# Two dense layers in float32 on one core: the second layer's products in seven block products for eight

## The chip, the cores and the metric

The kernel runs on one core of a Trainium2 chip. The metric is the device time of one execution in microseconds (us). An execution consists of one program on five engines: TensorE (PE, with the weight loads listed apart as PEld), VectorE (DVE), ScalarE (ACT), GpSimd (POOL, not used here) and SyncE (SP, which issues all the DMAs).

## The reference

Chunked attention with a few memory keys makes 3072 rows of 512 numbers; two dense layers with different activations follow. Only the second of them is touched by the change.

```python
x = attention(q, k, v, mem_k, mem_v)          # (3072, 512)
h = x @ moe_w_in                              # (3072, 2048)
g = h * (1.0 / (1.0 + np.exp(-1.702 * h)))
x = g @ moe_w_out                             # (3072, 512)
h = x @ moe2_w_in                             # (3072, 2048)
g = np.maximum(h, 0.0) + alpha * np.minimum(h, 0.0)
return (g @ moe2_w_out).astype(np.float32)    # (3072, 512)
```

The layers' weights and alpha arrive as float64.

## The kernel before

**Precision.** A float32 product is made of three products of numbers in the short format fp32r: each operand is split into a high part (a cast on ACT) and a low part (the difference, on DVE), and high x high, high x low and low x high are added in PSUM. So each block product costs three matmuls, and each operand that a product reads costs one cast and one subtraction. The matmuls that carry the time have 128x128 weights and 512 columns.

**Steps.** `steps` (lines 426 to 434) lists 192 steps: 6 blocks of 512 tokens by 16 chunks `f` of 128 hidden units in the first layer, and the same in the second. A step is `mm1` (12 matmuls into `h`, line 334), the activation (`act1`, lines 342 and 343, or `act2`, lines 348 and 349), `split_g` (lines 355 and 356), and one step later the second product: `mm2_t` (line 364) in the first layer, `mm2_n` (line 374) in the second, 12 matmuls into the PSUM pairs `ya` and `yb`. So a step of either layer has 24 matmuls, and the second layer has 2304. Attention for later tokens is spread over the first five blocks of the first layer (`attend`).

**Weights.** All 16 chunks of a layer stand in SBUF. A chunk comes by two DMAs as float64 (`w_load`), ACT takes the absolute value (`w_abs`, line 98), DVE builds the float32 out of the bits in four operations (`w_bits`, lines 106 to 115), then comes the split into high and low (`w_high`, line 126, `w_low`, line 131). The second layer's chunks are prepared in the last block of the first layer and shortly after it (lines 531 to 535), each into the buffers of a chunk of the first layer that is no longer used.

**Between the layers.** The first layer's result goes to DRAM (`y1`); the second layer loads blocks of 512 tokens of it (`load_y`) and splits them (`split_y`, lines 422 and 423). At the end of a block `finish2` moves the four accumulators out of PSUM and stores the rows.

**Order.** The code is written in program order; a scheduler of the framework then sets each engine's own order when the program is built. An engine works strictly down its own list, and waits where an operand isn't ready.

Of the kernel before, what the change touches and what calls it, by code (L numbers as in the profile page):

```python
# [9 lines left out]
F32 = mybir.dt.float32  # L10
# [21 lines left out]
P2_BLOCKS = [512] * 6  # L32
TBM = 512
# [12 lines left out]
NACC = (4, 5, 6, 7)  # L46
F64_TINY = float(np.uint32(0x38000000).view(np.float32))
# [4 lines left out]
def fused_kernel(ctx: ExitStack, tc: tile.TileContext, qs, ks, vs, ident, w_in1, w_out1, w_in2, w_out2, alpha, out):  # L52
# [3 lines left out]
    wp = ctx.enter_context(tc.tile_pool(name="wp", bufs=NF - 2 - NWB))  # L56
    wr = ctx.enter_context(tc.tile_pool(name="wr", bufs=2))
    xp = ctx.enter_context(tc.tile_pool(name="xp", bufs=2))
# [8 lines left out]
    y1 = dr.tile([NKC, 128, NT], F32, name="y1")  # L67

# [5 lines left out]
    pieces = [(p, f) for p in (1, 2) for f in range(NF)]  # L74
# [6 lines left out]

    def w_load(s):
        p, f = pieces[s]
        wi, wo = (w_in1, w_out1) if p == 1 else (w_in2, w_out2)
# [34 lines left out]
    def w_high(s):  # L119
        p, f = pieces[s]  # L120
        if f >= NF - 2 and "wp" not in side:
            side_stack.close()
            side["wp"] = side_stack.enter_context(tc.tile_pool(name="wp2", bufs=2, side="right"))
        pool = side["wp"] if f >= NF - 2 else side["wpb"] if f >= NF - 2 - NWB else wp
        wt[p, f] = [pool.tile([128, 2, 512], F32R, tag=t, name=f"{t}{p}_{f}") for t in ("whi", "wlo")]
        nc.scalar.copy(wt[p, f][0].rearrange("p i n -> p (i n)"), wst[s][1].bitcast(F32))  # L126
# [34 lines left out]


# [125 lines left out]
    def a_xcopy(m):  # L288
        tok = m * SQ
        b = int(np.searchsorted(p1_start, tok, side="right")) - 1  # L290
        if b not in xt:
            xt[b] = xp.tile([128, 2, NKC, TBM], F32R, tag="x", name=f"x{b}")
# [53 lines left out]
    def act2(h, n, f):  # L346
        t = gp.tile([128, TBM], F32, tag="t", name="t")
        nc.vector.tensor_scalar(out=t[:, :n], in0=h[:, :n], scalar1=0.0, scalar2=al_sb[:, f:f + 1], op0=ALU.min, op1=ALU.mult)  # L348
        nc.vector.scalar_tensor_tensor(out=t[:, :n], in0=h[:, :n], scalar=0.0, in1=t[:, :n], op0=ALU.max, op1=ALU.add)  # L349
        return t  # L350
# [18 lines left out]
    def mm2_n(p, y, gs, n, f):  # L369
        gh, gl = gs  # L370
        wh, wl = wt[p, f]
        for m in range(n // 128):
            for i, (g, w) in enumerate(((gh, wh), (gh, wl), (gl, wh))):
                mm = nc.tensor.matmul(  # L374
                    y[m], g[:, m * 128:(m + 1) * 128], w[:, 1, :],
                    start=(f == 0 and i == 0), stop=(f == NF - 1 and i == 2),
                )
                if ahead_done and f == NF - 1:
                    tc.keep_in_program_order(mm)

# [9 lines left out]
    def finish2(y, t0, n):  # L390
        last = t0 + n == NT
        if last:
            wide = ph2["pool"].tile([128, NKC, TBM], F32, tag="yraw", name="olast")
        for m in range(n // 128):
            o = wide[:, m] if last else op.tile([128, DM], F32, tag="o", name="o2")
            rows = out[t0 + m * 128:t0 + (m + 1) * 128, :]
            if last and m == n // 128 - 1:
                c = DM // 2
                nc.vector.tensor_copy(o[:, :c], y[m][:, :c])
                nc.scalar.copy(o[:, c:], y[m][:, c:])  # L400
                nc.sync.dma_start(out=rows[:, :c], in_=o[:, :c])
                nc.sync.dma_start(out=rows[:, c:], in_=o[:, c:])
                continue
            if m % 2:
                nc.scalar.copy(o, y[m])
            else:
                nc.vector.tensor_copy(o, y[m])
            nc.sync.dma_start(out=rows, in_=o)

    yraw = {}  # L410
    ph2 = {}

    def load_y(j):
        t0, n = j * P2_BLOCKS[0], P2_BLOCKS[j]
        t = ph2["pool"].tile([128, NKC, TBM], F32, tag="yraw", name=f"yraw{j}")
        nc.sync.dma_start(out=t, in_=y1[:, :, t0:t0 + n].rearrange("k p t -> p k t"))
        yraw[j] = t

    def split_y(j):
        t = yraw.pop(j)  # L420
        x = xp.tile([128, 2, NKC, TBM], F32R, tag="x", name=f"yx{j}")
        nc.scalar.copy(x[:, 0], t)
        nc.vector.tensor_tensor(out=x[:, 1], in0=t, in1=x[:, 0].bitcast(F32), op=ALU.subtract)
        xt[100 + j] = x
# [6 lines left out]
    t0 = 0  # L431
    for j, n in enumerate(P2_BLOCKS):
        steps += [(2, j, t0, n, f) for f in range(NF)]
        t0 += n
# [5 lines left out]
    ahead = []  # L440
    ahead_done = []
# [41 lines left out]
    side["wpb"] = ctx.enter_context(tc.tile_pool(name="wpb", bufs=NWB))  # L483
# [4 lines left out]
    def do_mm2(i):  # L488
# [13 lines left out]
    for i, (p, j, t0, n, f) in enumerate(steps):  # L502
# [83 lines left out]
```

## Time and profile before

| | |
|---|---|
| median of 3 runs | 1164.79 us (1162.69 to 1165.32) |
| the profiled execution: time | 1164.72 us |
| its span | 1162.9 us |
| TensorE busy | 1135.7 us, 98% of the span |
| VectorE busy | 590.6 us, 51% |
| ScalarE busy | 315.1 us, 27% |

The span counts from the first to the last thing that the profiler saw of the program; 1.8 us lie around it. Shares of busy time are means over stages: until about 150 us attention starts and the first layer's weights are prepared; until about 540 us the first layer and attention run side by side; from 540 to about 690 us the second layer's weights are prepared; from then on only the second layer runs. A matmul's recorded duration is longer than the distance to the next one, since matmuls are pipelined; distances are taken from start times.

### The profile page before, as it was taken

Reading aid. Unit: us, or ns where it says so; the run is one execution under the profiler, and the core shown is the slowest. Engines: PE = TensorE matmul, PEld = TensorE weight load, DVE = VectorE, ACT = ScalarE, POOL = GpSimd, SP = SyncE. Lnnn points to the kernel's source line nnn. Section 1 sums busy time; section 2 is a strip of 40 time slices with the busy share of each in tenths; the row PEclk is TensorE's granted clock in tenths of the full one; section 3 lists DMA queues with packets and bytes.
Section 4 is the critical chain, followed back from the end, with each engine's and each line's share of the span. In section 5 each row is a group of like instructions: output and inputs, shape, how many; then the busy total and the mean of one; then the engine's idle time right before and its main releaser. Section 6 shows DMA issues by size and latency. Waiting matters only on the chain.

```text
span 1162.9 us, 17787 instructions
## 1 busy us (share of the span) xinstructions
PE 1135.7 (98%) x7804; PEld 922.4 (79%) x7804; DVE 590.6 (51%) x848; ACT 315.1 (27%) x519; POOL 0.2 (0%) x4
## 2 busy tenths in 40 slices
PE   5799999999999999999999999999999999999998
PEld 4677778878878887888877888888888888888886
DVE  5899644343434333343799865334334434444443
ACT  3566432232222222223444321111111111111111
POOL 0000000000000000000000000000000000000000
PEclk6799999999999999999999999999999999999999
DMA  8754222121113112214444501001100100100001
GB/s 296 249 173 166 79 80 67 43 79 46 60 41 103 43 46 76 62 43 136 162 173 145 181 1 37 37 1 37 37 1 1 37 1 1 37 1 1 36 1 37
DMA packets 44382, 82.74 MB, mean 71 GB/s; under 512 B 5137, under 2 KB 21905, under 8 KB 44305
## 3 DMA queue, kind: packets, MB, share of 16 engines
q1 hardware_dynamic: 44304, 81.61, 20.8%
q8 instruction: 61, 1.00, 0.4%
q14 instruction: 17, 0.13, 0.0%
HBM read 69.02 MB, written 12.58 MB: 70 GB/s over the span
## 4 chain that ended last, share of the span: by engine, by line
PE 83%; DVE 8%; DMA 4%; ACT 2%; issue 1%; SPq 1%; DVEq 0%; ACTq 0%
PE h L334 40%; PE yb L374 11%; PE ya L374 11%; PE ya L364 9%; PE yb L364 8%; DMA wraw<-w_out 4%; PE xp L282 2%; DVE wtmp L112 2%; DVE wtmp L115 2%; PE sc L204 1%; DVE wlo L131 1%; DVE wtmp L106 1%; ACT wtmp L98 1%; DVE wtmp L109 1%; DVE gl L356 1%
## 5 line engine op out<-in xcount | busy, mean ns | idle before, releaser
L334 PE MATMUL h<-x,whi 128*128 128x512 f32 x768 | 244.6, 396 | 3.3 <-ACT whi L126 1.9
L355 ACT CAST gh<-t 128x512 fp32r<-128x512 f32 x192 | 119.0, 621 | 452.0 <-DVE t L349 329.0
L334 PE MATMUL h<-yx,whi 128*128 128x512 f32 x768 | 238.5, 390 | 0.0
L356 DVE TENSOR_TENSOR gl<-t,gh 128x512 fp32r<-128x512 f32 x192 | 132.3, 689 | 111.7 <-ACT gh L355 110.2
L334 PEld LDWEIGHTS h<-x,whi 128*128 128x128 f32 x768 | 143.3, 189 | 35.8 <-ACT whi L126 2.6
L348 DVE TENSOR_SCALAR t<-h,al_sb 128x512 f32<-128x512 f32 x96 | 71.9, 749 | 192.9 <-PE h L334 192.9
L334 PEld LDWEIGHTS h<-yx,whi 128*128 128x128 f32 x768 | 144.2, 188 | 30.9
L334 PE MATMUL h<-x,wlo 128*128 128x512 f32 x384 | 151.4, 394 | 0.0
L343 DVE SCALAR_TENSOR_TENSOR t<-t,h 128x512 f32<-128x512 f32 x96 | 65.8, 685 | 168.6 <-ACT t L342 168.3
L334 PE MATMUL h<-yx,wlo 128*128 128x512 f32 x384 | 149.8, 390 | 0.0
L342 ACT ACTIVATE t<-h 128x512 f32<-128x512 f32 x96 | 57.3, 598 | 187.2 <-PE h L334 186.9
L334 PEld LDWEIGHTS h<-x,wlo 128*128 128x128 f32 x384 | 72.4, 189 | 16.0 <-DVE wlo L131 0.4
L334 PEld LDWEIGHTS h<-yx,wlo 128*128 128x128 f32 x384 | 72.1, 188 | 15.5
L364 PE MATMUL ya<-gl,whi 128*128 128x512 f32 x192 | 77.2, 402 | 0.0
L364 PE MATMUL ya<-gh,whi 128*128 128x512 f32 x192 | 76.4, 398 | 0.3 <-ACT gh L355 0.3
L364 PE MATMUL yb<-gh,wlo 128*128 128x512 f32 x192 | 75.5, 393 | 0.0
L364 PE MATMUL yb<-gl,whi 128*128 128x512 f32 x192 | 75.4, 393 | 0.0
L364 PE MATMUL yb<-gh,whi 128*128 128x512 f32 x192 | 75.4, 393 | 0.0
L364 PE MATMUL ya<-gh,wlo 128*128 128x512 f32 x192 | 75.1, 391 | 0.0
L374 PE MATMUL ya<-whi,gh 128*128 128x512 f32 x192 | 74.9, 390 | 0.0
L374 PE MATMUL yb<-whi,gl 128*128 128x512 f32 x192 | 74.9, 390 | 0.0
L374 PE MATMUL yb<-whi,gh 128*128 128x512 f32 x192 | 74.9, 390 | 0.0
(67 smaller groups left out, 1298.2 us busy)
## 6 DMA issues: line engine op xcount, KB each, us to landing
wraw<-w_in SPq DMA_DIRECT2D x32, 512.0 KB, 4.0
wraw<-w_out SPq DMA_DIRECT2D x32, 512.0 KB, 4.9
v<-vs SPq DMA_DIRECT2D x24, 512.0 KB, 3.7
k<-ks SPq DMA_DIRECT2D x24, 416.0 KB, 4.5
q<-qs SPq DMA_DIRECT2D x24, 256.0 KB, 3.0
y<-o SPq DMA_DIRECT2D x24, 256.0 KB, 2.3
yraw<-y SPq DMA_DIRECT2D x6, 1024.0 KB, 5.3
out<-o SPq DMA_DIRECT2D x20, 256.0 KB, 2.1
```

What stands on the lines that cost most here:

```text
L98: i = nc.scalar.activation(out=a.bitcast(F32), in_=wst[s][0][:, :, 1].bitcast(F32), func=AF.Abs)
L112: nc.vector.scalar_tensor_tensor(out=a, in0=top, scalar=0xC0000000, in1=a, op0=ALU.bitwise_and, op1=ALU.bitwise_or)
L115: nc.vector.scalar_tensor_tensor(out=a, in0=low, scalar=29, in1=a, op0=ALU.logical_shift_right, op1=ALU.bitwise_or)
L282: nc.tensor.matmul(x[half[z], g, j, c * CHUNK:(c + 1) * CHUNK], s["v"][half[g], c, 2 * j + z, :], s["p"][half[g], 2 * z + j // 2, b * CHUN ...
L334: nc.tensor.matmul(h[:, :n], w[:, 0, k * 128:(k + 1) * 128], x[:, z, k, :n], start=(i == 0), stop=(i == 3 * NKC - 1))
L342: nc.scalar.activation(out=t[:, :n], in_=h[:, :n], func=AF.Tanh, scale=1.702 / 2)
L343: nc.vector.scalar_tensor_tensor(out=t[:, :n], in0=t[:, :n], scalar=1.0, in1=h[:, :n], op0=ALU.add, op1=ALU.mult)
L348: nc.vector.tensor_scalar(out=t[:, :n], in0=h[:, :n], scalar1=0.0, scalar2=al_sb[:, f:f + 1], op0=ALU.min, op1=ALU.mult)
L355: nc.scalar.copy(gh[:, :n], g[:, :n])
L356: lo_eng.tensor_tensor(out=gl[:, :n], in0=g[:, :n], in1=gh[:, :n].bitcast(F32), op=ALU.subtract)
L364: nc.tensor.matmul(y[m][:, :n], w[:, 1, m * 128:(m + 1) * 128], g[:, :n], start=(f == 0 and i == 0), stop=(f == NF - 1 and i == 2),)
L374: mm = nc.tensor.matmul(y[m], g[:, m * 128:(m + 1) * 128], w[:, 1, :], start=(f == 0 and i == 0), stop=(f == NF - 1 and i == 2),)
```

## The change

The second layer runs over 3 pairs of 512-token blocks (1024 tokens) in place of 6 blocks. Both its products are cut into 2x2 blocks and made by Strassen's method in seven block products, `p1` to `p7`, where eight were needed. This takes sums and differences of blocks of both operands ahead of the products, and sums of products behind them.

- **Weights** (`c_load` to `c_store`): during blocks 2 to 4 of the first layer, 16 units (8 of `w_in2`, 8 of `w_out2`) of four 128x256 blocks are loaded, converted as before, turned into seven combinations (four sums `s1` to `s4` of 128x256), split, and stored in DRAM (`wi2`, `wo2`). A unit's work is spread over three steps (`PSTEP`). The preparation in the last block of the first layer falls away.
- **Tokens** (`x_load`, `x_sum`, `x_split`): four blocks of `y1` make seven left operands per pair by four subtractions, seven casts and seven low parts. For pairs 1 and 2 these 11 steps are put between the products of the second product of the pair before (`fill`).
- **First product** (`first`): per pair 8 chunk pairs `fp` x 7 products x 6 matmuls. Accumulators `x`, `y`, `z` take up several products one after the other; ACT copies intermediate values out (`snap`), DVE adds them to the later ones, and the activation runs in SBUF.
- **Second product** (`second`): per pair 7 products x 4 quarters `jj` x 12 matmuls. `r_make` makes an operand for each (product, quarter): for p5, p6, p7 and p4 a subtraction of 128x1024 in place (lines 596 to 602), then a cast on ACT (line 605) and a low part on DVE (line 606), two quarters ahead of the product (`RLEAD`), into a ring of four slots.
- **Weights again** (`s_ahead`): the combinations are read from DRAM anew for each pair, in 60 units of up to 512 KB, ten units ahead.
- The output is written transposed and turned on the host.

```diff
-P2_BLOCKS = [512] * 6
+PAIR = 1024
...
+    def c_bits(u):
+        raw, oa = prep[u]
+        top, low, a, af = raw[:, :, :, 1], raw[:, :, :, 0], oa[:, :, 1].bitcast(U32), oa[:, :, 1].bitcast(F32)
+        nc.vector.tensor_scalar(out=af, in0=af, scalar1=F64_TINY, scalar2=F64_HUGE, op0=ALU.max, op1=ALU.min)
...
+    def c_sums(u):
...
+        for o, x, y, fn in ((s1, a21, a22, ALU.add), (s2, s1, a11, ALU.subtract), (s3, a11, a21, ALU.subtract),
+                            (s4, a12, s2, ALU.subtract)):
+            nc.vector.tensor_tensor(out=o, in0=x, in1=y, op=fn)
+        prep[u] += ob
+        for t in (oa[:, 1:4], ob[0], ob[1]):
+            nc.scalar.copy(t[:, :, 0], t[:, :, 1].bitcast(F32))
...
+    PRODUCTS = ("p1", "p5", "p6", "p3", "p7", "p2", "p4")
...
+    def x_sum(P, n):
+        x, y = {"p7": ("p3", "p5"), "p5": ("p5", "p1"), "p6": ("p3", "p5"), "p4": ("p2", "p6")}[n]
+        nc.vector.tensor_tensor(out=xraw[n], in0=xraw[x], in1=xraw[y], op=ALU.subtract)
...
+        nc.scalar.copy(hi, r)
+        nc.vector.tensor_tensor(out=lo, in0=r, in1=hi.bitcast(F32), op=ALU.subtract)
...
+            nc.sync.dma_start(out=t.bitcast(F32), in_=src)
...
+            w = units[P, "a", fp, d // 2][:, d % 2]
+            hi, lo = xops[P][n]
+            i = 0
+            for k in range(2):
+                for c, x in ((0, hi), (0, lo), (1, hi)):
+                    nc.tensor.matmul(
+                        to, w[:, c, k * 128:(k + 1) * 128], x[:, k], start=(i == 0 and n not in ADDED), stop=(i == 5),
...
+                with_, f, th = {"p3": ("u2", fp, 1), "p7": ("s5", fp + NFP, 1), "p2": ("s1", fp, 0), "p4": (None, fp + NFP, 0)}[n]
+                out = graw[f // 2, th][:, f % 2]
+                if with_ is not None:
+                    nc.vector.tensor_tensor(out=out, in0=to, in1=kept[with_], op=ALU.add)
+                    to = out
+                act2(out, to, f)
...
+    def r_make(P, d, jj):
...
+        if n == "p5":
+            nc.vector.tensor_tensor(out=b11, in0=b12, in1=b11, op=sub)
+        elif n == "p6":
+            nc.vector.tensor_tensor(out=b11, in0=b22, in1=b11, op=sub)
+        elif n == "p7":
+            nc.vector.tensor_tensor(out=b12, in0=b22, in1=b12, op=sub)
+        elif n == "p4":
+            nc.vector.tensor_tensor(out=b11, in0=b21, in1=b11, op=sub)
...
+        hi, lo = r_slot(P, f"r{P}_{d}_{jj}_")
+        nc.scalar.copy(hi, src)
+        nc.vector.tensor_tensor(out=lo, in0=src, in1=hi.bitcast(F32), op=sub)
...
+            for ahead in order[(0 if q == 0 else q + RLEAD):q + RLEAD + 1]:
+                r_make(P, *ahead)
+            if fill and q >= 4 and q % 2 == 0:
+                fill.pop(0)()
...
-        q = i - last1 - LAG
-        if q >= 0:
-            goal = NPC + 1 + (q * 3) // 4
-            while wtick[0] < min(2 * NPC + 1, goal):
-                w_tick(2 * NPC)
...
+        u, r = divmod(i - PREP0, PSTEP)
+        for v in (u, u - 1):
+            k = r + PSTEP * (u - v)
+            if 0 <= v < 2 * NFP and k < len(PREP):
+                for fn in PREP[k]:
+                    fn(v)
```

What this does to the order is shown at three places. In each row the line is that of the kernel it belongs to, then come the output, the inputs and the shape; numbers behind names tell buffers apart.

VectorE, in the first layer beside attention, before: `t` is the activation of a step, `gl` its low part, `x4` a low part of attention's result.

```order
L343 SCALAR_TENSOR_TENSOR t_3728<-t_3728,h1_3715 128x512
L356 TENSOR_TENSOR gl_3732<-t_3728,gh_3731 128x512
L343 SCALAR_TENSOR_TENSOR t_3767<-t_3767,h1_3754 128x512
L356 TENSOR_TENSOR gl_3771<-t_3767,gh_3770 128x512
L297 TENSOR_TENSOR x4_3613<-xp17_3786,x4_3613 128x2x4x64
```

VectorE, the same stage after: `t` and `gl` are lines 416 and 428, `oa11` is unit 11 of the weights (lines 199 to 206), `mx13`, `ex13` and `sm13` belong to attention's softmax.

```order
L416 SCALAR_TENSOR_TENSOR t_2875<-t_2875,h1_2862 128x512
L199 TENSOR_SCALAR oa11_4759<-oa11_4759 128x4x256
L428 TENSOR_TENSOR gl_2879<-t_2875,gh_2878 128x512
L298 TENSOR_REDUCE mx13_2826<-sc13_2793 128x8
L200 TENSOR_SCALAR oa11_4759<-oa11_4759 128x4x256
L306 TENSOR_TENSOR ex13_2827<-sc13_2793,mx13_2826 128x512
L203 SCALAR_TENSOR_TENSOR oa11_4759<-raw11_4709,oa11_4759 128x4x256
L325 TENSOR_REDUCE sm13_2830<-ex13_2827 128x8
L206 SCALAR_TENSOR_TENSOR oa11_4759<-raw11_4709,oa11_4759 128x4x256
L328 TENSOR_SCALAR sm13_2830<-sm13_2830 128x8
L416 SCALAR_TENSOR_TENSOR t_2923<-t_2923,h1_2910 128x512
```

Between the activation of one step and that of the next now stand four operations of 1024 columns of a weights' unit.

VectorE, in the second layer before: three operations a step, one after the other.

```order
L348 TENSOR_SCALAR t_7675<-h2_7662,al_sb_82 128x512
L349 SCALAR_TENSOR_TENSOR t_7675<-h2_7662,t_7675 128x512
L356 TENSOR_TENSOR gl_7679<-t_7675,gh_7678 128x512
L348 TENSOR_SCALAR t_7707<-h2_7694,al_sb_82 128x512
L349 SCALAR_TENSOR_TENSOR t_7707<-h2_7694,t_7707 128x512
```

VectorE, in pair 0 after, where the first product ends and the second begins: `g` are the activations, `acc7` the accumulator of the last chunk pair, `xr1` the token operands of pair 1 (`fill`), `r0_2_0` and `r0_2_1` the low parts for quarters 0 and 1 of p6; the two `rx` rows are those for quarter 2 of p6 and, last, for quarter 3 of p1.

```order
L478 TENSOR_TENSOR xr1p7_6825<-xr1p3_6824,xr1p5_6822 128x1024
L606 TENSOR_TENSOR r0_2_0_1_6953<-g0_0_0_6198,r0_2_0_0_6952 128x1024
L422 SCALAR_TENSOR_TENSOR g0_7_1_6213<-g0_7_1_6213,t_6793 128x512
L422 SCALAR_TENSOR_TENSOR g0_3_0_6204<-g0_3_0_6204,t_6804 128x512
L606 TENSOR_TENSOR r0_2_1_1_6973<-g0_1_0_6200,r0_2_1_0_6972 128x1024
L478 TENSOR_TENSOR xr1p5_6822<-xr1p5_6822,xr1p1_6821 128x1024
L602 TENSOR_TENSOR g0_0_0_6198<-g0_4_0_6206,g0_0_0_6198 128x1024
L421 TENSOR_SCALAR t_6815<-acc7_6747,al_sb_82 128x512
L606 TENSOR_TENSOR rx_6820<-g0_2_0_6202,rx_6820 128x1024
L602 TENSOR_TENSOR g0_1_0_6200<-g0_5_0_6208,g0_1_0_6200 128x1024
L606 TENSOR_TENSOR rx_6820<-g0_3_0_6204,rx_6820 128x1024
```

The low part for p1's last quarter stands behind three of p6, two subtractions for p4 and two sums for the next pair.

TensorE, in the second layer before: second products of one chunk, then first products of the chunk after the next.

```order
L374 MATMUL yb_7054<-whi2_12_5965,gh_7408 128x512
L374 MATMUL yb_7054<-wlo2_12_5966,gh_7408 128x512
L374 MATMUL yb_7054<-whi2_12_5965,gl_7409 128x512
L334 MATMUL h2_7456<-yx2_6696,whi2_14_6087 128x512 x2
L334 MATMUL h2_7456<-yx2_6696,wlo2_14_6088 128x512
```

TensorE, in pair 0 after, at the same place as the VectorE rows: the first row is quarter 2 of p5, lines 557 are the last product (p4) of the first product, `u35` is the weights' unit of p1's last quarter, `r0_2_0` is p6.

```order
L629 MATMUL acc9_6919<-rx_6820,u38_6764 128x512 x7
L557 MATMUL acc7_6747<-xw0_1_5937,u31_6638 128x512
L557 MATMUL acc7_6747<-xlo0p4_6159,u31_6638 128x512
L557 MATMUL acc7_6747<-xw0_1_5937,u31_6638 128x512 x2
L557 MATMUL acc7_6747<-xlo0p4_6159,u31_6638 128x512
L557 MATMUL acc7_6747<-xw0_1_5937,u31_6638 128x512
L629 MATMUL acc9_6919<-rx_6820,u38_6764 128x512 x5
L629 MATMUL acc8_6842<-rx_6820,u35_6711 128x512 x12
L629 MATMUL acc8_6842<-r0_2_0_0_6952,u40_6807 128x512
```

TensorE comes to p1's last quarter right behind three quarters of p5, and all of p6 stands behind it.

## Rows read from the trace of the kernel before

**Rows 1.** The page: busy us, share of span and instructions of each engine.

```profile
PE 1135.7 (98%) x7804; PEld 922.4 (79%) x7804; DVE 590.6 (51%) x848; ACT 315.1 (27%) x519; POOL 0.2 (0%) x4
```

**Rows 2.** Windows: busy us and count by engine, PE clock, DMA share, GB/s.

```profile
50.00:150.00 100.00, 97.56 (x790) 75.26 (x786) 86.03 (x116) 56.17 (x116) 0.00 (x0) 1.00 0.43 143
350.00:400.00 50.00, 50.00 (x462) 40.68 (x461) 21.28 (x40) 14.21 (x24) 0.00 (x0) 1.00 0.25 78
700.00:800.00 100.00, 100.00 (x441) 82.32 (x440) 42.50 (x59) 14.69 (x22) 0.00 (x0) 1.00 0.06 22
```

**Rows 3.** The chain that ended last: same place in two second-layer blocks (start, us).

```profile
726.70 5.48 PE h L334 x24
814.19 5.48 PE h L334 x24
```

**Rows 4.** The same chain: the same place in two first-layer blocks.

```profile
299.47 3.85 PE h L334 x17
398.80 3.85 PE h L334 x17
```

**Rows 5.** Timeline of PE (start, us) in the last block of the first layer.

```profile
598.10 0.39 PE L364 MATMUL yb<-gh,wlo 128*128 128x512 f32 x1
598.84 0.73 PE L334 MATMUL h<-x,whi 128*128 128x512 f32 x2 [0.36 <-DVE t L343]
...
620.94 0.40 PE L334 MATMUL h<-x,wlo 128*128 128x512 f32 x1
622.37 0.73 PE L334 MATMUL h<-x,whi 128*128 128x512 f32 x2 [1.03 <-DVE t L343]
```

**Rows 6.** Groups by line and shape: count, busy us, mean ns, idle before, releaser.

```profile
L356 DVE TENSOR_TENSOR gl<-t,gh 128x512 fp32r<-128x512 f32 x192 | 132.3, 689 | 111.7 <-ACT gh L355 110.2 <-ACT whi L126 1.1
L348 DVE TENSOR_SCALAR t<-h,al_sb 128x512 f32<-128x512 f32 x96 | 71.9, 749 | 192.9 <-PE h L334 192.9
L131 DVE TENSOR_TENSOR wlo<-wtmp,whi 128x1024 fp32r<-128x1024 f32 x32 | 38.9, 1217 | 0.6 <-ACT whi L126 0.5
L106 DVE TENSOR_SCALAR wtmp<-wtmp 128x1024 f32<-128x1024 f32 x32 | 22.0, 689 | 21.0 <-ACT wtmp L98 20.7
```

**Rows 7.** Timeline of DVE where its list never runs dry.

```profile
599.31 1.22 DVE L131 TENSOR_TENSOR wlo<-wtmp,whi 128x1024 fp32r<-128x1024 f32 x1
600.44 1.22 DVE L112 SCALAR_TENSOR_TENSOR wtmp<-wraw,wtmp 128x1024 uint32<-128x1024 uint32 x1
601.58 0.69 DVE L356 TENSOR_TENSOR gl<-t,gh 128x512 fp32r<-128x512 f32 x1
602.18 0.68 DVE L343 SCALAR_TENSOR_TENSOR t<-t,h 128x512 f32<-128x512 f32 x1
```

**Rows 8.** Windows around the fall and the rise of PE's clock.

```profile
4.00:6.00 2.00, 0.98 (x66) 0.72 (x64) 0.14 (x2) 0.00 (x0) 0.00 (x0) 1.00 0.89 270
6.00:8.00 2.00, 0.00 (x0) 0.00 (x0) 1.41 (x3) 0.48 (x1) 0.00 (x0) 0.85 0.98 302
8.00:10.00 2.00, 0.00 (x0) 0.00 (x0) 0.86 (x2) 0.14 (x1) 0.00 (x0) 0.50 1.03 392
...
44.00:46.00 2.00, 2.00 (x8) 1.62 (x7) 2.00 (x4) 0.00 (x0) 0.00 (x0) 0.77 0.00 0
```

**Rows 9.** Timeline of PE ahead of that rise.

```profile
41.26 1.63 PE L334 MATMUL h<-x,whi 128*128 128x512 f32 x3
42.69 0.63 PE L334 MATMUL h<-x,wlo 128*128 128x512 f32 x1
43.12 1.05 PE L334 MATMUL h<-x,whi 128*128 128x512 f32 x2
```

**Rows 10.** Windows: stretches with much DMA traffic.

```profile
10.00:12.00 2.00, 0.00 (x0) 0.00 (x0) 0.00 (x0) 1.12 (x1) 0.00 (x0) 0.50 1.03 412
640.00:650.00 10.00, 10.00 (x46) 8.28 (x45) 6.53 (x9) 2.03 (x3) 0.00 (x0) 1.00 0.74 260
585.00:600.00 15.00, 14.64 (x65) 11.73 (x64) 13.79 (x17) 8.78 (x12) 0.00 (x0) 1.00 0.52 172
```

More of the change, by code (lines that the diff above doesn't have):

```diff
@@ L388, in finish1 @@
             nc.sync.dma_start(out=y1[m, :, t0:t0 + n], in_=o[:, :n])
[L390 to L402, printed above, removed]
-                continue
[L404 to L408, printed above, removed]
@@ new lines, in s_done, with two_banks, g_alloc, snap @@
+    def s_done(n):
+        streamed[1] += n
+        s_ahead(streamed[1] + 10)
+    npair = [0]
+    def two_banks():
+        t = pair(("a", "ya", "yb")[npair[0] % 3], f"acc{npair[0]}")
+        npair[0] += 1
+        return t
+    graw = {}
+    def g_alloc(P):
+        for j in range(NFP):
+            for th in range(2):
+                graw[j, th] = chunk_slot(6 + 2 * (j % 4) + j // 4, th, DIM, F32, f"g{P}_{j}_{th}")
+    def snap(src, tag, name):
+        t = gp.tile([128, TBM], F32, tag=tag, name=name, bufs=2)
+        nc.scalar.copy(t, src)
+        return t
@@ L426, in fused_kernel @@
+    late = {}
+    ringx = []
     steps = []
@@ L529, in fused_kernel @@
             attend(j, 2 * f + 2)
-        q = i - last1 - LAG
-        if q >= 0:
-            goal = NPC + 1 + (q * 3) // 4
-            while wtick[0] < min(2 * NPC + 1, goal):
-                w_tick(2 * NPC)
-        if i == last1 + 6:
-            split_y(0)
-            load_y(1)
-        if p == 2 and f == 6 and j + 1 < len(P2_BLOCKS):
-            split_y(j + 1)
-            if j + 2 < len(P2_BLOCKS):
-                load_y(j + 2)
-    for i in range(len(steps) - LAG, len(steps)):
-        do_mm2(i)
+        u, r = divmod(i - PREP0, PSTEP)
[4 more added lines that the diff above has]
+                    fn(v)
+        if i == last1 + 2:
+            x_load(0)
+            fill = x_steps(0)
+        if i >= last1 + 4 and fill:
+            fill.pop(0)()
+        if last1 + 4 <= i:
+            s_ahead(i - last1 - 4)
+    s_ahead(10)
+    for P in range(NPAIR):
+        g_alloc(P)
+        for fp in range(NFP):
+            first(P, fp, (lambda: do_mm2(len(steps) - 1)) if P == 0 and fp == 0 else None)
+        if P == 0:
+            ringx.append(xp.tile([128, 2, 2, 2, TBM], F32R, tag="x1", name="rx"))
+        fill = []
+        if P + 1 < NPAIR:
+            x_load(P + 1)
+            fill = x_steps(P + 1)
+        second(P, fill)
+        npair[0] += 1
+        while fill:
+            fill.pop(0)()
 def _layout(q, k, v, mem_k, mem_v):
```

265 lines of the change are left out of this document (206 added, 59 removed).

## Prediction

> **What bounds the kernel now.** I read the page's first part, then the windows by stage, then the chain that ended last, then single instructions. TensorE is busy for 98% of the span, VectorE for 51% [rows 1]. The share is a mean, so the stages count: from 350 to 400 us and from 700 to 800 us TensorE is never idle at its full clock, and VectorE is busy for 43% of each [rows 2]. The chain of waits says the same: the piece of line 334 with 24 matmuls that starts at 726.70 comes again at 814.19 [rows 3], so a block of the second layer takes 87.49 us for 16 x 24 = 384 matmuls, 0.2278 us each, and nothing else stands between them. A block of the first layer takes 99.33 us [rows 4]; what it has beyond that is attention's matmuls. The second layer thus goes by the number of its matmuls: 2304 x 0.2278 = 524.8 us. TensorE waits for VectorE only where the second layer's weights are prepared [rows 5].
>
> **The part removed.** Seven products for eight: per pair, the first product has 8 x 7 x 6 = 336 matmuls, the second 7 x 4 x 12 = 336; three pairs make 2016. 288 fewer, all with 512 columns and a new 128x128 weight load as now, at 0.2278 us: **-65.6 us**. They go entirely, since TensorE is the bound there. Left are 459.2 us.
> [...]
>
> The second layer's preparation leaves the last block of the first layer. There TensorE lost time twice: from 598.10 to 598.84 and from 620.94 to 622.37, where a matmul's step is 0.23 [rows 5], so 0.51 + 1.20 = **-1.7 us** (0 if the eleven steps for pair 0's token operands, now at that place, cost as much).
>
> **The part moved: weights in the first layer.** A unit costs VectorE four operations for the bits, four sums of 256 columns and three low parts. Two-input operations of 1024 columns last 1.217 us, of 512 columns 0.689, single-input ones of 1024 columns 0.689 [rows 6]; where the list is full, each starts 0.09 before the one ahead has ended: 1.13 us from start to start for 1024 columns, 0.60 for 512 [rows 7]. So 2 x 1.13 + 2 x 0.60 for the bits, 4 x 0.4 for the sums (estimated by the line through 512 and 1024 columns), 0.87 + 2 x 0.60 for the low parts: 7.1 us. A unit takes three steps, 3 x 99.33 / 16 = 18.6 us, in which VectorE already does 43% [rows 2], 8.0 us: together 15.1, 81%. The 16 units fill 49 steps, 304 us. In the order, a unit's operations stand between the activation of one step and that of the next, where TensorE has the second product of the step before as cover, 12 matmuls or 2.7 us. Nearest row: from 50 to 150 us VectorE was busy for 86%, and TensorE idle for 2.44 of 100 us [rows 2], with the first layer's weights prepared in the same way. So 0 to 7.4 us in 304; I take **+3 us**. ACT's and SP's share (3.2 us of casts, and 2.8 MB per unit in the queue ahead of attention's loads) lies beside it.
>
> **The part added in the first product.** Per chunk pair TensorE has 42 matmuls, 9.57 us. VectorE has three sums, four first and four second operations of the activation, 3 x 0.60 + 3 x 0.40 + 0.66 + 4 x 0.60 = 6.1 us. (0.40 is an estimate for a 512-column single-input operation in SBUF with a scalar per row: half of what line 106 does, and the 0.06 by which line 348 is longer than a plain one; from PSUM line 348's 0.749 less 0.09 [rows 6].) TensorE's order interleaves three chunk pairs, so a wait for a sum has four or more products of 1.37 us in between. Cost nothing; if the cover fails, some 0.3 us each, inside the range.
>
> **The part added in the second product.** This decides. Over a pair VectorE has 28 low parts and 16 subtractions of 1024 columns, and in pairs 0 and 1 eleven more for `fill`: 55 x 1.13 = 62 us, with eight evictions 67, beside 76.5 us of TensorE. The sum fits, but not everywhere. Take the stretch from the first matmul of p1 to p1's last quarter. TensorE passes 36 matmuls of p1, 24 of the first product's end and 36 of p5, and one with the high part, before it needs the low part: 97 x 0.2278 = **22.1 us**. VectorE's list up to that low part (the last row of the fourth order shown), counted from the subtraction for p5's quarter 2, is 34 operations: 17 of 1024 columns, 3 sums, 7 second and 5 first operations of the activation, and 2 first ones from PSUM: 17 x 1.13 + 10 x 0.60 + 5 x 0.40 + 2 x 0.66 = **28.5 us**. It starts about 1.2 us before p1 does: the four operations ahead of it, 2.7 us, follow on the end of p3 of chunk pair 6, 18 matmuls before p1. So the low part comes at 28.5 - 1.2 + 0.1 = 27.4, and TensorE waits **5.3 us**. All of p6 stands behind this wait on TensorE. With full durations in place of steps VectorE needs 31.6, starts 0.9 ahead, and the wait is 8.6, with 1 more at p6 and p3; if VectorE runs ahead, 0. I take 5.3, the full list being the case of [rows 7]. Pair 1 has the same operations in that stretch. Pair 2 has no `fill` and one part less of several: 12 x 1.13 + 10 x 0.60 + 5 x 0.40 + 0.66 = 22.3, less 1.2, under 22.1: no wait (with durations 1.8).
> [...] Some 9 matmuls at 0.2 more: 1.8 us a time. I count it in pairs 0 and 1, since these rows show the fall behind a single idle time of a few us: **2 x (5.3 + 1.8) = +14.2 us** (0 to 22.8).
>
> **Sum.** 1164.7 (the profiled execution, 0.1 from the median of the runs) - 65.6 - 1.7 + 3 + 14.2 = **1115 us**. The tail stays: copies out of PSUM and a last store. Bounds: all covered, 1097; all at their upper ends and the 1.7 not regained, 1164.7 - 65.6 + 7.4 + 22.8 + 1.8 = 1131.
>
> **Rivals.**
> Covered: VectorE's list is no bound anywhere, since its total is below TensorE's in each product; 1097 to 1104. For it speaks the 81 to 88% of both sums; against it the count of 34 operations.
> More late places: beside p1's last quarter also the starts of blocks in the first layer and the pairs' ends wait, and TensorE's clock falls there too. With the upper bounds and three more waits with a fall of the clock, 3 x (1 + 1.8) = 8.4, 1131 + 8 = 1139. For it speaks [rows 5]: VectorE full, TensorE waits.
> The other side: the weights' stream is the bound. Per pair 29.4 MB of units, 2.1 of tokens and 2.1 of output, 100.7 MB in all. At TensorE's pace that is 100.7 / 459 = 219 GB/s, where now nearly nothing moves. From 585 to 600 us the queue moved 172 GB/s [rows 10]; at that rate the layer takes 585 us, 61 more than now, and the kernel 1164.7 - 1.7 + 3 + 61 = 1227. It decides below 192 GB/s, where the layer is as long as now. Against it: 260 GB/s at 74% of the DMA engines and 412 at full [rows 10], with ten units ahead.
> That the matmuls aren't saved is no case: 2016 are in the program.
>
> **How the numbers follow.** Forecast 0.56 (1105 to 1125), covered 0.14, more late places 0.22, stream 0.05, no change or slower by some mixture 0.03 (waits of 50 us and more in all). The range, 8 in 10: from the covered case's 1099 to the third case's 1139. Faster by over 0.2% (about what a measurement of this kernel can tell from no change) 0.92, within 0.2% 0.02, slower 0.06.
>
> **What would show it.** In the profile after: second-layer matmuls at 0.228 us; one wait of TensorE of about 5 us for line 606, in pairs 0 and 1 only, followed by matmuls at 0.43; no wait over 1 us in blocks 2 to 4 of the first layer. Wrong it would be if the waits lie at weights' units (line 517), at ACT's copies, or if pair 2 is as long as the others.

## The result: about 1% slower

The changed kernel takes 1175.54 us (median of 6 runs, 1173.28 to 1178.81) against 1164.62 us of the kernel before: a ratio of 1.0095, 95% interval 1.007 to 1.012. The forecast was 1115 us, 1099 to 1139. The profiled execution has a span of 1177.0 us, the one of before 1162.9 us. It is the longest of the six (1178.81 us), so the ledger below adds up to 14.1 us, where the medians differ by 10.9.

### The profile page after: what moved, and what is told of

Its sections match the earlier page's. It is cut to its first block, busy times and chain, and to the rows that moved or that the text cites. A ratio compares the mean times of both kernels' runs of the same rounds, so it can differ in the third digit from the quotient of the medians.

```text
span 1177.0 us, 18312 instructions
## 1 busy us (share of the span) xinstructions
PE 1098.4 (93%) x7516; PEld 876.2 (74%) x7516; DVE 762.5 (65%) x1090; ACT 408.1 (35%) x633; POOL 0.2 (0%) x4
## 4 chain that ended last, share of the span: by engine, by line
PE 64%; DVE 17%; DMA 12%; issue 3%; ACT 3%; SPq 1%; DVEq 0%; ACTq 0%
PE acc L629 19%; PE acc L557 14%; PE h L407 13%; PE ya L436 7%; PE yb L436 6%; DMA u<-wi 3%; PE hz L557 3%; DMA wo<-oa 2%; DMA wi<-oa 2%; DMA wraw<-w_out 2%; DVE ob L217 1%; DVE wtmp L123 1%; DVE wtmp L126 1%; DVE oa L203 1%; DVE t L416 1%
## 5 line engine op out<-in xcount | busy, mean ns | idle before, releaser
L629 PE MATMUL acc<-rx,u 128*128 128x512 f32 x504 | 127.9, 401 | 13.6 <-DVE rx L606 9.4
L629 PE MATMUL acc<-r,u 128*128 128x512 f32 x504 | 125.4, 396 | 5.1 <-ACT k L541 5.1
L557 PE MATMUL acc<-xh,u 128*128 128x512 f32 x384 | 128.3, 392 | 0.4 <-ACT s L541 0.4
L629 PEld LDWEIGHTS acc<-rx,u 128*128 128x128 f32 x504 | 97.1, 193 | 37.0 <-DVE rx L606 10.3
L629 PEld LDWEIGHTS acc<-r,u 128*128 128x128 f32 x504 | 94.1, 188 | 29.8 <-ACT k L541 7.6
L428 DVE TENSOR_TENSOR gl<-t,gh 128x512 fp32r<-128x512 f32 x96 | 66.0, 688 | 36.7 <-ACT gh L427 35.2
L427 ACT CAST gh<-t 128x512 fp32r<-128x512 f32 x96 | 59.6, 621 | 84.4 <-DVE t L416 74.9
L557 PE MATMUL acc<-xw,u 128*128 128x512 f32 x240 | 85.7, 390 | 0.0
L557 PEld LDWEIGHTS acc<-xh,u 128*128 128x128 f32 x384 | 72.1, 188 | 17.9 <-DVE g L422 1.7
L407 PEld LDWEIGHTS h<-x,wlo 128*128 128x128 f32 x384 | 73.2, 191 | 16.1 <-DVE wlo L141 0.3
L541 ACT COPY s<-acc 128x512 f32<-128x512 f32 x48 | 28.3, 590 | 116.2 <-PE acc L557 114.0
```

The costliest lines, as they stand in the source:

```text
L407: nc.tensor.matmul(h[:, :n], w[:, 0, k * 128:(k + 1) * 128], x[:, z, k, :n], start=(i == 0), stop=(i == 3 * NKC - 1))
L427: nc.scalar.copy(gh[:, :n], g[:, :n])
L428: lo_eng.tensor_tensor(out=gl[:, :n], in0=g[:, :n], in1=gh[:, :n].bitcast(F32), op=ALU.subtract)
L541: nc.scalar.copy(t, src)
L557: nc.tensor.matmul(to, w[:, c, k * 128:(k + 1) * 128], x[:, k], start=(i == 0 and n not in ADDED), stop=(i == 5), skip_group_check=n in ADDED,
L629: nc.tensor.matmul(to[:, m], w[:, ft, c, m * 128:(m + 1) * 128], g[:, ft], start=(jj == 0 and ft == 0 and i == 0 and n not in ADDED), stop ...
```

## The profile after, and where the time went

The first part of the page, as in [rows 1]: busy us, share of the span and instructions of each engine.

```profile
PE 1098.4 (93%) x7516; PEld 876.2 (74%) x7516; DVE 762.5 (65%) x1090; ACT 408.1 (35%) x633; POOL 0.2 (0%) x4
```

TensorE has its 288 matmuls fewer, but where it was busy for 98% it is now busy for 93%: 79 us idle instead of 27. To find the stages I take one mark that both kernels have, VectorE's first eviction at the end of each block of the first layer (line 447, in the kernel before line 387, `o<-ya`). In the kernel before the first four of these lie 99.3 us apart. After, they are at 153.66, 267.90, 382.76, 490.88, 592.33 and 678.14. The last one, before and after:

```profile
639.18 0.68 DVE L387 TENSOR_SCALAR o<-ya 128x512 f32<-128x512 f32 x1
```

```profile
678.14 0.69 DVE L447 TENSOR_SCALAR o<-ya 128x512 f32<-128x512 f32 x1 [1.66 <-PE ya L436]
```

Windows between the marks (busy us and count by engine, PE's clock, DMA share, GB/s), of after:

```profile
153.66:267.90 114.24, 101.23 (x818) 77.94 (x817) 87.46 (x147) 47.35 (x75) 0.00 (x0) 0.93 0.66 231
267.90:382.76 114.86, 102.74 (x844) 81.73 (x844) 83.76 (x141) 46.00 (x72) 0.00 (x0) 0.95 0.62 222
382.76:490.88 108.12, 106.74 (x1001) 85.47 (x1001) 40.15 (x69) 29.98 (x50) 0.00 (x0) 0.97 0.27 87
490.88:592.33 101.45, 101.45 (x918) 82.28 (x917) 46.31 (x72) 32.51 (x52) 0.00 (x0) 1.00 0.17 53
678.14:1177.03 498.89, 470.33 (x2003) 375.82 (x2001) 348.25 (x443) 151.33 (x190) 0.00 (x0) 0.98 0.61 191
```

and the last stretch of before:

```profile
639.18:1162.94 523.76, 519.42 (x2281) 427.68 (x2279) 238.18 (x326) 83.19 (x122) 0.00 (x0) 1.00 0.08 27
```

The time is lost twice. **First layer:** the mark at its end comes 39.0 us later than before (678.14 - 639.18). Two blocks took 15 us more than 99.3, the third 9, with idle time and a clock below 1; from 490.88 to the last mark TensorE is never idle again. Ten of the 288 saved matmuls lie ahead of the mark (288 less 2281 - 2003), 2.3 us, so the real loss is 41.3 us. **Second layer:** 2003 matmuls at 0.2278 are 456.3 us, and with the 4.2 us that before needs beyond its matmuls at the end (523.76 - 2281 x 0.2278) it would be 460.5. It took 498.89: 38.4 us lost. Sum: -65.6 + 41.3 + 38.4 = +14.1, which is the difference of the two spans.

**What TensorE waited for in the first layer.** Who waited for whom, from 100 to 500 us of after (us, times, longest):

```profile
DVE oa L199 <- ACT oa L193: 53.0, 15, 6.6
ACT oa L193 <- DMA wo<-oa: 24.1, 7, 7.2
ACT oa L193 <- DMA wi<-oa: 19.6, 6, 4.9
PE ya L436 <- ACT gh L427: 16.8, 6, 5.9
ACT oa L193 <- DMA wi<-ob: 8.3, 2, 4.4
```

Line 193 is `c_abs`, the first step of a unit's conversion. It writes `oa`, and `oa` and `raw` share two buffers; so unit u+1 cannot begin until the stores of unit u (line 232) have read their buffer. ACT waits 52 us for that in all (24.1 + 19.6 + 8.3; the 8.3 the profile puts down to the stores of `ob`, which stand between the two of `oa`). One such place, first ACT, then VectorE, then TensorE (start, us; in brackets the idle time before it and who ended it):

```profile
299.42 0.60 ACT L415 ACTIVATE t<-h 128x512 f32<-128x512 f32 x1
307.24 1.12 ACT L193 ACTIVATE oa<-raw 128x1024 f32<-128x1024 f32 x1 [7.23 <-DMA wo<-oa]
308.26 0.61 ACT L427 CAST gh<-t 128x512 fp32r<-128x512 f32 x1
```

```profile
301.16 0.68 DVE L416 SCALAR_TENSOR_TENSOR t<-t,h 128x512 f32<-128x512 f32 x1
308.39 0.69 DVE L199 TENSOR_SCALAR oa<-oa 128x1024 f32<-128x1024 f32 x1 [6.55 <-ACT oa L193]
```

```profile
305.40 0.39 PE L407 MATMUL h<-x,wlo 128*128 128x512 f32 x1
308.92 0.50 PE L436 MATMUL ya<-gh,whi 128*128 128x512 f32 x1 [3.13 <-ACT gh L427]
310.48 0.63 PE L436 MATMUL ya<-gh,wlo 128*128 128x512 f32 x1
```

VectorE had the activation's `t` ready at 301.84. The cast `gh` that needs it takes 0.61 us, but stands behind line 193 in ACT's list, and ACT did not take it ahead of that: it starts at 308.26, 6.42 us after `t` was ready, and TensorE, whose cover ended with the matmul of 305.40, waits 3.13 us. Then the matmuls last 0.63 in place of 0.39: the granted clock is 0.50 from 309.8 to 313.2. The profile shows it at 0.50 in seven such stretches, 34 us in all, between 183 and 392 us.

The pace is not the one of the code either. `PSTEP` says three steps for a unit; the first and the last line 193 are at

```profile
130.80 1.15 ACT L193 ACTIVATE oa<-raw 128x1024 f32<-128x1024 f32 x1
371.77 1.14 ACT L193 ACTIVATE oa<-raw 128x1024 f32<-128x1024 f32 x1 [4.82 <-DMA wo<-oa]
```

that is 16.1 us a unit with all waits in it. In the order of ACT's instructions they stand behind the 14th, 16th, 19th, 21st tanh and so on to the 47th, one in 2.2 steps or 13.6 us, where the code issues them behind the 34th to the 79th: the scheduler had moved them up.

**What it waited for in the second layer** (TensorE's waits from 640 us on):

```profile
PE acc L629 <- DVE rx L606: 9.4, 2, 5.1
PE acc L629 <- ACT k L541: 5.1, 5, 1.2
PE hz L557 <- DMA u<-wi: 4.8, 8, 1.5
PE acc L629 <- ACT rx L605: 4.3, 2, 2.1
```

The place that the forecast named, p1's last quarter in pair 0:

```profile
773.35 0.50 PE L629 MATMUL acc<-rx,u 128*128 128x512 f32 x1 [2.14 <-ACT rx L605]
778.93 5.06 PE L629 MATMUL acc<-rx,u 128*128 128x512 f32 x11 [5.08 <-DVE rx L606]
785.15 1.20 PE L629 MATMUL acc<-r,u 128*128 128x512 f32 x4 [1.16 <-ACT k L541]
```

Eleven matmuls take 5.06 us behind the wait, nine of them 0.43 us from the one ahead: the granted clock is 0.50 from 774.1 to 784.2 us. VectorE's list is full there, as the forecast had it. From the start of p1 (748.89) to the end of the low part that TensorE waits for, 30.0 us later, VectorE is idle for 1.65 us, 1.27 of them ahead of a sum that waits for a load of the next pair's tokens:

```profile
767.84 1.23 DVE L478 TENSOR_TENSOR xr1p<-xr1p,xr1p 128x1024 f32<-128x1024 f32 x1 [1.27 <-DMA xr1p<-y]
777.66 1.22 DVE L606 TENSOR_TENSOR rx<-g,rx 128x1024 fp32r<-128x1024 f32 x1
```

The third row of TensorE's is one that no term of the forecast has: p6 adds into the banks of p1, so it waits until the copies of p1's result (line 541) are out.

## Experiments on the first layer

Two theories. **Buffer:** the absolute value waits for the stores of the unit before and holds ACT's list. **Pace:** units come closer than VectorE's list can bear, whatever the buffers. A third, that the stores' traffic itself costs, goes with the first run. The measure is the mark at the end of the first layer: 678.14 us in the change. Each mark is that of one profiled execution.

**Without the preparation.** In place of `c_load` to `c_store` each unit stores halves of the first layer's weights:

```
-    PREP = [[c_load], [c_abs, c_bits], [c_sums], [c_store]]
+    PREP = [[c_plain]]     # four stores per unit from whi and wlo, kept in program order
```

> Leaves out the loads, conversion and sums of the second layer's weights; halves of the first layer's weights are stored in their place, a unit every three steps, in the same sizes (14.7 MB in all), and read back in the second layer as before. If it is the preparation's chain of loads, ACT and VectorE work that holds TensorE in the first layer (whichever link of it), blocks 1 to 4 are back at about 99 us each, some 44 us less in all: 1129 to 1136 us. If the stores' traffic in DRAM and in the DMA queue is what costs, most of the loss stays: above 1160 us. The second layer stays as it is, with its waits of 24 us.

Measured: 1137.08 us, ratio to before 0.9764 (0.9746 to 0.9781), 1 us over the range expected. The mark:

```profile
633.82 0.69 DVE L453 TENSOR_SCALAR o<-ya 128x512 f32<-128x512 f32 x1 [1.66 <-PE ya L442]
```

So the preparation costs 44.3 us in the first layer (678.14 - 633.82). TensorE's idle time and its clock account for it: between 100 and 400 us it is idle for 28.9 us in the change and for 2.4 here, and half of the 34 us at a granted clock of 0.50 is lost, which makes 43.5. The stores are all there (29.4 MB; the expectation says 14.7), spaced as in the code, and the first four marks are 99.3 us apart again: the stores' traffic is not it. The loads of the second layer's weights are left out here; that their traffic isn't it either is told by the runs below with a place kept and the third buffer, which have loads and stores and are 3.1 and 5.5 us over this one.

**The third buffer.**

```
-        raw = wr.tile([128, 4, 512], U32, tag="wraw", name=f"raw{u}", bufs=2)
+        raw = wr.tile([128, 4, 512], U32, tag="wraw", name=f"raw{u}", bufs=3)
     (the same for oa, wraw and xw; OPB = 2 in place of 3 makes room)
```

> A third buffer for the units' raw and converted values (one output buffer of three given up for it), so that a unit's conversion no longer has to wait until the stores of the unit before have left. Nothing pins the units' pace: in the order they now come every 1.6 steps where it was 2.2. Buffer theory (ACT's absolute value waits for the stores' DMA, 52 us in all, and holds tanh and casts behind it): these waits vanish and at least 30 of the 44 us come back, 1135 to 1147 us. Pace theory (VectorE is given more per step than it can do beside the activation): nothing comes back, or it gets worse, 1170 to 1190 us, with TensorE waiting for VectorE's t or gl in place of ACT's cast.

Measured: 1159.15 us, 0.9943 (0.9917 to 0.9968); the mark is at 664.34. Neither theory's range. The scheduler used the freedom to put the units closer still: the first absolute value is at 126.27, the last at 300.27, 11.6 us a unit. Line 193 still waits, now for loads and for one store, 20.4 us in all (2.8 of them in issue, 1.7 for a load of attention's):

```profile
ACT oa L193 <- DMA raw<-w_out: 6.6, 4, 2.6
ACT oa L193 <- DMA raw<-w_in: 5.3, 4, 2.5
ACT oa L193 <- DMA wo<-oa: 4.0, 1, 4.0
```

So taking the buffer's wait away alone tells little, because the order changed with it. Two more things are different. From 125 to 310 us VectorE is busy for 92%; and with two output buffers for three (`OPB`) an eviction waits 4.38 us for a store and holds a cast of attention's (line 369), for which TensorE then waits:

```profile
125.00:310.00 185.00, 168.72 (x1412) 132.11 (x1412) 170.15 (x282) 92.10 (x142) 0.00 (x0) 0.94 0.82 287
```

```profile
372.67 0.60 ACT L445 ACTIVATE o<-yb 128x512 f32<-128x512 f32 x1 [4.38 <-DMA y<-o]
373.80 1.65 PE L407 MATMUL h<-x,whi 128*128 128x512 f32 x3 [4.64 <-ACT x L369]
```

How the loss of this run divides between these is not shown.

**The absolute value kept at its place.**

```
-        nc.scalar.activation(out=oa[:, :, 1].bitcast(F32), in_=..., func=AF.Abs)
+        tc.keep_in_program_order(nc.scalar.activation(out=oa[:, :, 1].bitcast(F32), in_=..., func=AF.Abs))
```

> One edit: ACT's absolute value of each unit is kept at the place where the code issues it, so that a unit comes every three steps (18.6 us), from step 33 to 78, where it came every 2.2 steps from step 14 on. Pace theory: VectorE is at 81% and TensorE hardly waits; first layer back to about 99 us a block, 1132 to 1140 us. Buffer theory: a unit's stores land 13.5 to 18.5 us after its absolute value, which fits in 18.6, so most of the 52 us of ACT's waits go too; up to 2 us may be left at some units, 1135 to 1148 us. If the load on VectorE itself is the cause whatever the pace, no gain: above 1165 us.

Measured: 1148.02 us, 0.9855 (0.9817 to 0.9894), at the upper end of the buffer theory's range; the mark is at 644.38, still 10.6 over the run without preparation. What is left is again line 193 behind a store, mainly at one place:

```profile
374.63 1.12 ACT L193 ACTIVATE oa<-raw 128x1024 f32<-128x1024 f32 x1 [7.77 <-DMA wi<-oa]
375.65 0.58 ACT L369 CAST x<-xp 128x512 fp32r<-128x512 f32 x1
377.13 0.86 PE L277 MATMUL sc<-k,q 64*32 64x64 f32 x64 [2.84 <-DVE x L370]
```

The units still come unevenly (at 341.15, 358.39, 374.63 and 400.95), and where two are 16 us apart the store is too late.

**Both edits.**

> Both edits at once: the absolute value kept at its place in the code (a unit every three steps) and the third buffer. If the pace and the buffer are two causes, each of which is left in the run with the other edit alone (there the last block of the first layer began its evictions at 664.3 us with the buffer, at 644.4 us with the place, against 678.1 us with neither and 633.8 us without the preparation), the first layer is now as without the preparation, 633 to 637 us, and the whole 1126 to 1140 us. If the place alone does all that can be done, 643 to 646 us and 1140 to 1149 us.

Measured: 1131.99 us, 0.9716 (0.9702 to 0.973); the mark is at 636.91, 3.1 over the run without preparation. ACT waits for a DMA ahead of line 193 once:

```profile
ACT oa L193 <- DMA raw<-w_out: 0.7, 1, 0.7
```

A part of this gain isn't the units': the third buffer serves the first layer's own weights too. Ahead of the first unit TensorE waits for them once, 1.9 us with two buffers and 0.6 with three (place kept, then both edits):

```profile
PE h L407 <- ACT whi L136: 1.9, 1, 1.9
```

```profile
PE h L407 <- DVE wlo L141: 0.6, 1, 0.6
```

So the preparation still costs some 3.1 + 1.3 = 4.4 us here.

**The same pace with two and with three buffers.** To set the buffer apart from the pace, units are issued and kept one in 2.2 steps, near the steps where the change's order had them, with two buffers and with three:

```
-PSTEP = 3
+ABS_AT = (13, 15, 18, 20, 22, 24, 26, 28, 30, 32, 35, 37, 39, 41, 44, 46)
...
-        u, r = divmod(i - PREP0, PSTEP)
+        for v in range(2 * NFP):
+            k = i - ABS_AT[v] + 1
```

> Two buffers as in the change, and the units issued and kept at the pace that they had in the change's order, one every 2.2 steps, from step 15 to 49. It should lose what the change loses: the first layer's last evictions begin at 670 to 680 us, 1167 to 1178 us in all, under either theory.

> The same pace of one unit every 2.2 steps, with the third buffer. If the wait for the stores is what costs at this pace, ACT no longer waits for them and most of the 44 us come back: last evictions of the first layer at 634 to 645 us, 1126 to 1140 us in all. If 13.6 us for a unit are too short for VectorE's 7.1 us beside its 43%, most of the loss stays: 655 us and more, 1147 to 1165 us.

Measured: two buffers 1154.38 us, 0.9917 (0.9891 to 0.9942), mark at 654.88; three buffers 1135.43 us, 0.9754 (0.9712 to 0.9796), mark at 639.27. Windows from 125 to 400 us, of the change, of two buffers and of three:

```profile
125.00:400.00 275.00, 246.74 (x2069) 192.53 (x2070) 201.69 (x333) 111.62 (x179) 0.00 (x0) 0.94 0.64 224
```

```profile
125.00:400.00 275.00, 260.39 (x2294) 204.44 (x2293) 208.59 (x343) 118.32 (x198) 0.00 (x0) 0.98 0.65 226
```

```profile
125.00:400.00 275.00, 268.50 (x2362) 214.63 (x2361) 212.78 (x352) 120.73 (x191) 0.00 (x0) 0.99 0.65 225
```

At the same pace the third buffer takes 15.6 of 21.1 us away (654.88 to 639.27, against 633.82), about 2 of them ahead of the units. The second of these marks is of an execution of 1132.55 us, near the shortest of four (1131.81 to 1142.58); the medians of the whole time differ by 19.0. VectorE does the most there (212.78 of 275 us, 77%), and TensorE loses the least: at this pace VectorE's load is not what costs. My expectation for two buffers missed: it loses 21.1 us and not 44. ACT waits 33.9 us for stores there against 52, but why these units, shifted by about a step, wait so much less than those of the change's own order I have not settled.

| run | us per unit in the order | buffers | mark | over no preparation |
|---|---|---|---|---|
| the change | 13.6 | 2 | 678.14 | 44.3 |
| third buffer | closer (11.6 in the trace) | 3 | 664.34 | 30.5 |
| near pace kept | 13.6 | 2 | 654.88 | 21.1 |
| place kept | 18.6 | 2 | 644.38 | 10.6 |
| near pace kept, third buffer | 13.6 | 3 | 639.27 | 5.5 |
| place kept, third buffer | 18.6 | 3 | 636.91 | 3.1 |

The rows with two buffers, and those with a place kept, are in line with one mechanism: a unit's chain from the absolute value to the landing of its stores is some 13.5 to 18.5 us in the change's trace (180.43 to 193.99, 148.17 to 166.65), and a spacing that is shorter than that, with two buffers, ends in ACT's list. The row of the third buffer alone it doesn't explain: 30.5 us are lost there with 4.0 us of waits for a unit's stores.

## Experiments on the second layer

**Without the next pair's token steps.**

```
-            x_load(P + 1)
-            fill = x_steps(P + 1)
+            xops[P + 1] = xops[P]
```

> Pairs 1 and 2 use pair 0's token operands: the loads of their tokens and the eleven steps on ACT and VectorE (twice) are left out, so the output is not the reference's. Theory that VectorE's list is too long at the start of the second product: TensorE's waits for lines 605 and 606 in pairs 0 and 1 (13.6 us, 14.5 with the restart, and about 4.4 us at half clock behind them) vanish, 1155 to 1160 us; pair 2 is unchanged and the short waits for line 541's copies (1.2 us each) stay. Rival (the activation and the order, not the token steps): the waits stay, above 1168 us.

Measured: 1156.31 us, 0.9928 (0.9913 to 0.9943). From the mark (676.68) to the end it takes 477.79 us where the change takes 498.89, and of TensorE's waits for lines 605 and 606 none is left:

```profile
PE acc L629 <- ACT k L541: 7.0, 6, 1.2
PE hz L557 <- DMA u<-wi: 2.1, 6, 0.6
```

So 21.1 us of the second layer's 38.4 are the token steps at the second product's start, and the clock does not fall there any more (1.00 granted in the mean behind the mark, 0.98 in the change). The size is good to a few us: in the four runs that have the change's second layer and two buffers (the change, no preparation, place kept, near pace kept) the stretch took 498.0 to 502.4 us. With the third buffer, which the token operands `xw` use too, it took 491.5 to 493.7.

**The same steps, later.** All work is kept; it only begins at p6's last quarter:

```
-            if fill and q >= 4 and q % 2 == 0:
+            if fill and q in (11, 12, 13, 14, 16, 18, 19, 20, 21, 22, 24):
     (x_sum and x_split kept in program order for pairs 1 and 2)
```

> The change as it is, but the eleven steps for the next pair's tokens are kept in the order of the code and begin with the last quarter of the third product (p6) in place of the second product's first quarter. Theory that VectorE's list at the start of the second product is too long: TensorE's waits for lines 605 and 606 (13.6 us) and the half clock behind them vanish as without these steps, 1155 to 1161 us. Rival, that VectorE has too much in the second product as a whole: the waits move to later products, above 1168 us.

Measured: 1157.2 us, 0.9929 (0.9912 to 0.9945). The stretch behind the mark is 476.71 us, with 8.2 us of waits in all (7.0 of them for the copies of line 541, there line 543), so it is as good as without the steps: the lists of VectorE and ACT are too long at one place, not in the whole product. The profiled execution is the shortest of four (1153.21 us). Which engine's list costs how much is not separated, since both runs take the steps away from both; in the change TensorE waits 9.4 us for VectorE and 4.3 for ACT.

**Without the stream of units.**

```
+            if i >= 10:
+                units[key] = slot[i % 10]
+                streamed[0] += 1
+                continue
```

> The second layer loads ten units of weights once and uses them for everything, so that nearly no weights' traffic is left there; the output is not the reference's. If the stream of units is no bound but only late at the starts of pairs, the waits for units (4.8 us, 6.0 with the restarts) vanish and all others stay: 1166 to 1171 us. If the stream is what slows the second layer (late tokens behind it in the queue, ACT's and VectorE's accesses), the waits for lines 605 and 606 go too: 1140 to 1156 us.

Measured: 1159.82 us, 0.9958 (0.9944 to 0.9971), between the two expectations. TensorE's waits there (the lines of this kernel are 6 further down):

```profile
PE acc L563 <- DVE g L578: 6.4, 3, 2.1
PE acc L635 <- ACT k L547: 5.0, 4, 1.4
PE acc L635 <- DVE rx L612: 0.4, 1, 0.4
```

The waits for units are gone, the wait for p1's low part nearly so, and there are new ones in the first product, for other sums. But the order is another too: with the loads gone the scheduler lets the first product reach to 59.7 us behind p1's start (743.10 to 802.76) where it was 21.0 (748.89 to 769.91), and that is cover for the low part. So this run doesn't tell what the stream does to that wait. That the stream need not be the cause is told by the run before this one: it has the whole stream and none of these waits.

## All three edits together

> The three edits together: place, third buffer, later token steps. The gains lie in different stages and should add up: 44 us in the first layer and some 19 in the second from the change's 1175.5, so 1112 to 1121 us. If the second layer's waits are only pushed to its other waits (copies, units), 1122 to 1135 us.

Measured: 1116.5 us (5 runs, 1114.09 to 1117.18), ratio to before 0.9579 (0.9566 to 0.9593). The page, and the window behind the mark:

```profile
PE 1076.4 (97%) x7516; PEld 867.8 (78%) x7516; DVE 761.4 (68%) x1090; ACT 408.8 (37%) x633; POOL 0.2 (0%) x4
```

```profile
638.28:1114.73 476.45, 463.87 (x2003) 373.70 (x2001) 348.14 (x443) 150.98 (x190) 0.00 (x0) 1.00 0.63 200
```

The same 7516 matmuls, the same work on VectorE and ACT, 59 us less than the change and 4.2% less than the kernel before. The gains add up: 39.9 us ahead of the mark (678.14 - 638.28), 22.4 behind it (498.89 - 476.45).

## Why the prediction was wrong, point by point

- **The part removed, -65.6 us:** right. 288 matmuls fewer at 0.2278 are what the ledger above and the last run need.
- **The last block of the first layer, -1.7:** 3.1 (5.4 between the marks of before and of the run without preparation, less the 2.3 of the matmuls moved), on the right side.
- **The weights in the first layer, +3 (0 to 7.4): this step failed; it was 44.3.** The price of VectorE's load was about right: with the place kept and the third buffer the preparation costs some 4.4 us (3.1 by the marks, and 1.3 that this buffer saves ahead of it), inside the step's bounds. Wrong were two sentences of the step. "A unit takes three steps, 18.6 us" was read off `PSTEP`; the order of the engines' instructions had a unit in 13.6 us, and 20 to 32 steps earlier than the code. And "ACT's and SP's share (...) lies beside it" took the casts' time and the loads' place in the queue, and left out what a unit's first ACT instruction must wait for: its output buffer, still being read by a store. In the place shown above that instruction waited 7.23 us, and `gh`, which stood behind it, started 6.42 us after its operand was ready. The forecast costed each instruction of the moved step, but not the reuse of its buffers. Its nearest row, the first layer's weights from 50 to 150 us, could not show that: there the absolute value goes into `wtmp`, whose last reader is VectorE, and nothing is stored.
- **The second product, +14.2 (0 to 22.8):** right in mechanism and place, mis-sized: 21.1, inside its bounds. TensorE's wait for line 606 was 5.08 and 4.28 us in pairs 0 and 1 where 5.3 was forecast. Ahead of it is another of 2.14 us for the cast of the same quarter (line 605), since in ACT's list too token steps stood ahead, and one of them (line 490, at 767.84) had waited 2.42 us for a tokens' load. The 1.8 us that the sum has behind each wait were an estimate from the trace of before: a granted clock of 0.50 behind idle time of a few us [rows 8], and 0.43 us a matmul ahead of the rise [rows 9]. No row there shows such a loss behind a wait; the change shows nine matmuls 0.43 us apart in pair 0, as forecast, and seven in pair 1, at a granted clock of 0.50: 1.8 and 1.4 us more than at 0.23 each.
- **What the sum did not have, 17.3 us:** what the run without token steps still loses in the second layer (477.79 - 460.5). Six waits for line 541's copies, 7.0 us; units late in the first product, 2.1; the rest, 8.2 us, worked out from the matmuls' starts: some 30 steps of 0.30 to 0.34 us in place of 0.23, about 3; a mean of 0.2293 us for the others, about 3; and about 2 in the steps that hold the waits. "None in pair 2" holds for lines 605 and 606; pair 2 has two of the copies' waits, 1.17 us each.
- **The rivals.** "More late places" named the right kind, with the clock's fall (to 0.50 granted), but priced three at 8.4 us where TensorE stood idle 17 times between 100 and 400 us, for 28.9 us. The stream as the bound is refuted: the change moved 191 GB/s behind the mark, below the 192 from which that rival was to decide, and the last run moved the same bytes at 200 GB/s and was 22 us faster, with 0.8 us of waits for units. The slower side came by a mechanism that was on no list.
- **Slips that decide nothing:** pair 2's list adds up to 22.2 us, not 22.3. The covered case is given as 1097 to 1104, but the range begins at 1099. That TensorE waits for VectorE only where the second layer's weights are prepared holds for 1.4 us in the trace of before; 3.4 us are waits for attention's `ex`.

The sum was 50 us under the time of before; without what the order and two buffers cost, it is what the last run shows: 1116.5 against 1115. That they agree so well is partly chance: 16.0 us of the second layer's losses are left (476.45 - 460.5) that the sum did not have, and the 14.2 that it had there are gone.

## What to carry to other kernels

Before costing work that is moved beside other work, look up where a scheduler puts it in each engine's list, and ask of each instruction what its output buffer waits for: an instruction that waits for a store's landing belongs behind, not ahead of, what the bounding engine needs next (here `gh` came 6.42 us late behind one). The two buffers that a load's and a result's tile share here tied a unit to the stores of the one before, for 52 us of ACT's waits in all. And a spacing that is written in the code holds only if something keeps it (18.6 us a unit in the code, 13.6 in the order).

## What the runs showed of the hardware

- A store's time to landing did not follow from how closely the units come. The 512 KB stores of `oa` into `wi2` took (median) 5.8 us in the change, 4.7 with the place kept, 3.4 with the third buffer alone, where the units are closest, and 3.2 with both:

```profile
wi<-oa SPq DMA_DIRECT2D x8, 512.0 KB, 5.8
```

```profile
wi<-oa SPq DMA_DIRECT2D x8, 512.0 KB, 4.7
```

```profile
wi<-oa SPq DMA_DIRECT2D x8, 512.0 KB, 3.4
```

```profile
wi<-oa SPq DMA_DIRECT2D x8, 512.0 KB, 3.2
```

  Those into `wo2` took 5.3, 6.0, 4.0 and 3.1. With the near pace kept it was 5.1 and 4.6 with two buffers, 3.1 and 4.8 with three. So most, not all, are shorter with the third buffer; why is not shown.
- A single wait of about 3 us cost 1.7 us more behind it at one place and 3.4 at another: behind the 3.13 us that end at 308.92 in the change, and the 2.84 us that end at 377.13 in the run with the place kept, the granted clock was 0.50 for 3.4 and 6.8 us (the 6.8 worked out from means of 0.99 from 372 to 379 and 0.52 from 379 to 386 us), with 0.43 us from matmul to matmul in place of 0.23; half of that, 1.7 and 3.4 us, is lost.
- In the second layer with its stream of units a matmul's step is 0.2294 us in the mean where nothing waits, 0.2278 in the kernel before; it is 0.2290 with the stream taken away, so the stream is not the main part of the difference. The cause is open.
